# Hash attention and a squared-ReLU layer: the first pair's features moved behind the first sum, the last chunk's stores moved off Pool's queue

## The chip, the cores and the metric

The kernel runs on one core of a Trainium2 chip. The metric is the device time of one launch in microseconds (us). A core has engines that run side by side, each with its own instruction queue: TensorE (PE in the profile, its weight loads PEld), VectorE (DVE), ScalarE (ACT), GpSimd (POOL) and SyncE (SP, which only issues DMAs here). DMAs are issued from the queues of SP, ACT and POOL.

## The reference

Four batches of eight heads, 768 positions, head dimension 64. A query may see a key only if both have the same six-bit hash; the bits are the signs of six projections. The result, 3072 rows of 512, goes through a layer with 2048 hidden units and a squared ReLU.

```
q_bits = einsum('bhsd,dk->bhsk', q, proj) > 0          # and k_bits
q_bucket = sum(q_bits * 2**arange(6))                  # and k_bucket
mask = q_bucket[..., :, None] == k_bucket[..., None, :]
scores = where(mask, q @ k.T / 8, -1e9)
attn = exp(scores - max) / (sum + 1e-9);  x = (attn @ v) as (3072, 512)
h = x @ w_in                                           # (3072, 2048)
out = (relu(h) ** 2) @ w_out                           # (3072, 512)
```

## The kernel before

**Attention.** The 32 heads are worked in 16 pairs (two heads fill 128 partitions). For a pair, `features` (L330) turns the loaded queries and keys with two DVE transposes of 128x768; `hash_bits` (L337) multiplies them with the projections on PE, and `signs` (L351) makes bits of them with eight ACT instructions. `weigh` (L379) scales the key bits on ACT. Keys come in six tiles of 128. `score(pr, kt)` (L386) forms the products of bits and of features for one key tile on PE, in two column pieces (512 and 256), and ACT takes the exponential of each piece; `add_up` (L419) sums the exponentials on DVE; `attend` (L432) multiplies them with the values on PE. `finish` and `normalize` divide by the sums.

PSUM pieces for scores, hash products and totals come from one ring of three tiles (`turn`, L104), so a piece must be read by ACT before the third next one is begun. The exponentials lie in a ring of four. Beside all this, one weight piece after another is split and rounded to float32 (`part_weight`, `place_power`, `round_weight` on DVE and ACT).

The first pair differs from the others. Its features are PE transposes. The features of pair 1 are made in it, as there is no earlier pair to make them in, and its `prepare()` (hash products and signs of the next pair, L610) stands between score tiles; in later pairs `prepare` is called from `finish`, and the features of the pair after are made at the pair's start.

**The layer.** It runs in three chunks of 1024 rows (`NCH`, L66), with both matrix products done by Strassen-like schemes: seven products of half-size blocks in place of eight. For w_in, `hidden` and `hidden_pair` go through units. For w_out, `project` (L1050) runs seven outer products k = 0 to 6, each made by `product` (L699) with seven groups of matmuls on three accumulators. Within `product`, ACT copies an accumulator between groups (`keep`, L713: one, two, five, three): the copy `one` must have read accumulator 0 before PE adds the third group into it. The other groups' callbacks c11, c12, c22, c21 make the sums on DVE. At the first use of each weight factor a later one is loaded (`load_leaf`, L988, on ACT's queue).

**The output.** Outer product k = 5 (`sixth`, L1097) completes the output blocks (0, 1) and (1, 1), each in two halves (`close`, L1063), and k = 6 (`fourth`, L1105) block (1, 0). `put_out` (L1014) transposes a half on DVE and stores it with four DMAs of 32 partitions. Before the change block (1, 1) is stored from POOL's queue in every chunk, the others from SP's; in the last chunk POOL also takes two of the four stores of the first half of block (1, 0). The second half of that block in the last chunk goes another way (`put_last`, L1030: transposes on PE, stores from SP and ACT). After k = 5 of the last chunk `guard` (L762) decides whether the inputs need the general version that follows in the program; every engine reads its answer (L1278) and branches past that version.

The order of instructions on each engine is that of the program text (`tc.manual_schedule()`, L584); waits between engines and for DMAs are put in by the framework.

Of the kernel before, what the change touches and what calls it, by code (L numbers as in the profile page):

```python
# [34 lines left out]
def kernel(  # L35
# [10 lines left out]
    nc = tc.nc  # L46
# [20 lines left out]
    NCHUNK = B * S // NCH  # L67
# [36 lines left out]
    def turn(name):  # L104

        return ps_s.tile([P, 2, 512], FP32, name=name, tag="turn")
# [279 lines left out]
    def score(pr, kt):  # L386

        e = ring[len(weights) % NRING]
        weights[pr, kt] = e
        key = slice(kt * P, (kt + 1) * P)  # L390
        sts = []

        def products(st, lo, hi, src, first):
            for h in range(2):
                rows = slice(h * D, (h + 1) * D)
                nc.tensor.matmul(  # L396
                    out=st[:, h, 0:hi - lo], lhsT=src[pr, 1][rows, key],
                    rhs=src[pr, 0][rows, lo:hi], start=first, stop=not first,
                )


        if (pr, kt) == (0, 0):
            for lo, hi in CUTS:
                sts.append(turn("st"))
                products(sts[-1], lo, hi, feat, True)
        for i, (lo, hi) in enumerate(CUTS):
            if len(sts) <= i:
                sts.append(turn("st"))
                products(sts[i], lo, hi, bits, True)
                products(sts[i], lo, hi, feat, False)  # L410
            else:
                products(sts[i], lo, hi, bits, False)
            nc.scalar.activation(  # L413
                out=e[:, :, lo:hi], in_=sts[i][:, :, 0:hi - lo], func=ACTF.Exp, scale=scale
            )
# [3 lines left out]
    def add_up(pr, kt):  # L419

        if kt == 1:
            totals[pr] = p_n.tile([P, 2, S], FP32, name="total")
            nc.vector.scalar_tensor_tensor(
                out=totals[pr], in0=weights[pr, 0][:, :, 0:S], scalar=SB * TINY,
                in1=weights[pr, 1][:, :, 0:S], op0=ALU.add, op1=ALU.add,
            )
        else:
            nc.vector.tensor_tensor(  # L428
                out=totals[pr], in0=totals[pr], in1=weights[pr, kt][:, :, 0:S], op=ALU.add
            )  # L430

    def attend(pr, kt):  # L432
        if kt == 0:
            outs[pr] = ps_o.tile([P, 1024], FP32, name="xo")
        xo = outs[pr]
        for lo, hi in (CUTS[0], (CUTS[1][0], S + 1)):
            for h in range(2):
                nc.tensor.matmul(  # L438
                    out=xo[h * D:(h + 1) * D, lo:hi],
                    lhsT=nat[pr, "v_nat"][:, h, kt * D:(kt + 1) * D],  # L440
                    rhs=weights[pr, kt][:, h, lo:hi],
                    start=(kt == 0), stop=(kt == SB - 1),
                )
# [4 lines left out]
    def sum_up(pr, tot):  # L448


        tot = tot[:, 0]
        srcs = [totals[pr]] + [weights[pr, SB - 1]] * (pr in sums)
        for src in srcs:
            for c in range(2):
                for h in range(2):
                    g = 2 * h + c
                    nc.tensor.matmul(  # L457
                        out=tot[g * 32:(g + 1) * 32, 0:HS], lhsT=ones,
                        rhs=src[:, h, c * HS:(c + 1) * HS],
                        start=src is srcs[0], stop=src is srcs[-1],  # L460
                    )
        flip = p_n.tile([P, HS], FP32, name="flip")
        nc.vector.transpose(out=flip, in_=tot[:, 0:HS])
        once = p_n.tile([P, NB], FP32, name="once")
        nc.vector.reciprocal(
            out=once, in_=flip.rearrange("p (n f) -> p n f", f=32)[:, :, 0]
        )
        both = p_n.tile([P, 2, NB], FP32, name="both")
        nc.vector.tensor_tensor(
            out=both, in0=which,  # L470
            in1=once.rearrange("p (o n) -> p o n", o=1).to_broadcast([P, 2, NB]), op=ALU.mult,
        )
        onces[pr] = both

    def spread(pr):

        both = onces.pop(pr)
        rec = outs[pr][:, 1024 - 2 * NB:]
        for h in range(2):
            nc.tensor.matmul(  # L480
                out=rec[h * D:(h + 1) * D], lhsT=picks[:, h * D:(h + 1) * D],
                rhs=both.rearrange("p c n -> p (c n)"), start=True, stop=True,
            )
        recs[pr] = rec
# [58 lines left out]
    def load_x(i):  # L543

        x = p_c.tile([P, NFT, NCH], FP32, name="x")
        nc.gpsimd.dma_start(out=x, in_=x_all[:, :, i * NCH:(i + 1) * NCH])
        xs[i] = x, [p_c.tile([P, 2, NCH // 2], FP32, name=f"t_x{n}") for n in range(3)]
# [16 lines left out]
    def sum_x(i, n):  # L564

        x, (t1, t2, t3) = xs[i]
        lo, hi = slice(0, NCH // 2), slice(NCH // 2, NCH)
        b11, b12, b21, b22 = x[:, 0:2, lo], x[:, 0:2, hi], x[:, 2:4, lo], x[:, 2:4, hi]
        minus(*((t1, b12, b11), (t2, b22, t1), (t3, b22, b12), (b12, b21, t2))[n - 1])

    def finish(pr, beside=None):

        tot = turn("tot")
        if beside:
            beside()
        sum_up(pr, tot)
        if pr == NP - 1:
            sum_x(0, 2)
            sum_x(0, 3)
        for kt in (SB - 2, SB - 1):  # L580
            attend(pr, kt)
        spread(pr)

    with tc.manual_schedule():  # L584
# [21 lines left out]
        for pr in range(NP):  # L606
            a, b = 2 * pr, 2 * pr + 1
            more = pr + 1 < NP

            def prepare():  # L610

                hash_bits(pr + 1, turn("hash"))
                for w in (1, 0):
                    signs(pr + 1, w)


            if pr + 2 < NP:
                load_pair(pr + 2)
            if pr == X_0:
                load_x(0)  # L620
            if not more:
                sums_in(3)
            if more and pr > 0:
                for w in range(2):
                    features(pr + 1, w)
            if pr > 0:
                round_weight(b - 2)
                load_weight(b)
            score(pr, 0)
            if pr == 0:  # L630
                first_keys(1, turn("hash"))
            score(pr, 1)
            if pr == 0:
                for w in range(2):
                    features(1, w)
            if pr > 0:
                finish(pr - 1, prepare if more else None)
            add_up(pr, 1)
            if pr > 0:
                normalize(pr - 1)  # L640


            if pr == X_0 + 1:
                for n in range(2):
                    load_unit(n)
            part_weight(a)
            score(pr, 2)
            if pr == 0:
                prepare()
            score(pr, 3)  # L650
            if more and pr > 0:
                weigh(pr + 1)
            place_power(a)
            attend(pr, 0)
            attend(pr, 1)
            for kt in (2, 3):
                add_up(pr, kt)
            if more:
                load_values(pr + 1)


            round_weight(a)
            part_weight(b)
            if more:
                load_weight(a + 2)
            score(pr, 4)
            score(pr, 5)
            if pr == 0:
                weigh(1)
            place_power(b)  # L670
            attend(pr, 2)
            attend(pr, 3)
            add_up(pr, 4)

            if pr not in sums:
                add_up(pr, 5)
            if pr in sums:
                sums_in(sums[pr])
# [335 lines left out]
        def put_out(i, ih, jh, n, o):  # L1014


            ot = p_r.tile([P, HN], FP32, name="h", bufs=NH)
            nc.vector.transpose(out=ot, in_=o)
            m0 = ih * HD + n * P
            at = slice(i * NCH + jh * HN, i * NCH + (jh + 1) * HN)  # L1020
            for a in range(P // 32):
                queue = nc.gpsimd if (ih, jh) == (1, 1) else nc.sync
                if (i, ih, jh) == (NCHUNK - 1, 1, 0) and a % 2:
                    queue = nc.gpsimd
                queue.dma_start(
                    out=out[at, m0 + a * 32:m0 + (a + 1) * 32].rearrange("(c i) j -> i c j", i=32),
                    in_=ot[a * 32:(a + 1) * 32].rearrange("i (c j) -> i c j", j=32),
                )
# [451 lines left out]
```

## Time and profile before

| what | value |
|---|---|
| three runs | 882.09, 882.37, 883.88 us; median 882.37 |
| the profiled execution | 882.09 us, of it 880.2 us from the first to the last instruction |
| busy: PE, DVE, ACT, POOL | 866.6, 756.0, 391.7, 106.9 us |
| mean granted clock | 0.997 |
| attention | until about 334 us |
| three chunks of the layer | the rest |
| last matmul of the last product begins / last store is issued | 870.9 / 873.8 us |

In the profile's lines an instruction has its engine, its line in the kernel, the tile that it writes and the tiles that it reads, and in brackets the idle time of its engine before it with what ended that idle time. Busy time is not limit time: an engine can be busy with work that nobody waits for, and a wait costs only where the chain to the end runs through it.

### The profile page before, as it was taken

The numbers are of one execution on the slowest core, as the hardware profiler recorded it, in microseconds if no ns is written. First come the engines' busy times: TensorE is split into PE (matmuls) and PEld (weight loads), VectorE is DVE, ScalarE is ACT, GpSimd is POOL, SyncE is SP. The second block draws the span as 40 slices with busy tenths as digits, with TensorE's granted clock in tenths as the row PEclk, the third lists the DMA queues.
The fourth block names the chain that finished last, engine by engine and source line by source line (L and its number), as shares of the span: only waits on it lengthen the run. The fifth ranks groups of instructions, "written<-read, shape, count | busy, mean of one in ns | idle before, by whom it ended". The sixth has DMA issues, their size and how long they took to land.

```text
span 880.2 us, 12164 instructions
## 1 busy us (share of the span) xinstructions
PE 866.6 (98%) x4364; PEld 519.7 (59%) x4364; DVE 756.0 (86%) x1096; ACT 391.7 (45%) x673; POOL 106.9 (12%) x172
## 2 busy tenths in 40 slices
PE   8999999999999999999999999999999999999996
PEld 3444444444444444444688865556888755568885
DVE  5999999999999998888779968888889788888875
ACT  6988888888888851222211123332111233321110
POOL 2000000000000000564221021111000211110002
PEclk9999999999999999999999999999999999999998
DMA  9677779889777545989897765436846744355565
GB/s 175 149 144 134 198 183 190 181 275 206 158 166 188 160 137 199 301 260 289 283 355 249 180 160 174 162 117 228 287 145 188 170 159 156 128 167 151 161 175 104
DMA packets 224132, 167.09 MB, mean 190 GB/s; under 512 B 164449, under 2 KB 181345, under 8 KB 224065
## 3 DMA queue, kind: packets, MB, share of 16 engines
q1 hardware_dynamic: 189152, 87.19, 40.4%
q0 software_dynamic: 12528, 41.30, 15.0%
q10 hardware_dynamic: 22384, 37.76, 13.9%
q8 instruction: 36, 0.59, 0.3%
q14 instruction: 32, 0.25, 0.1%
HBM read 124.52 MB, written 41.68 MB: 189 GB/s over the span
## 4 chain that ended last, share of the span: by engine, by line
PE 94%; DVE 2%; ACT 1%; DMA 1%; issue 0%; ACTq 0%; DVEq 0%
PE acc L708 40%; PE st L396 17%; PE acc L927 16%; PE xo L438 13%; PE acc L880 5%; PE tot L457 2%; PE hash L346 2%; DVE total L428 1%; DMA k_nat<-in_k_dram 1%; ACT e L413 1%; ACT bits L356 1%; DMA w_in<-s_in 0%; DVE out_piece L179 0%; DVE power L171 0%; ACT small L160 0%
## 5 line engine op out<-in xcount | busy, mean ns | idle before, releaser
L413 ACT ACTIVATE e<-st 128x1024 f32<-128x1024 f32 x192 | 145.1, 810 | 46.8 <-PE st L396 42.7
L396 PE MATMUL st<-feat,feat 64*128 64x512 f32 (+1 forms) x768 | 150.4, 483 | 0.0
L438 PE MATMUL xo<-e,v_nat 128*64 128x512 f32 (+1 forms) x768 | 134.8, 492 | 0.0
L708 PE MATMUL acc<-b,leaf 128*128 128x256 f32 x600 | 133.3, 379 | 0.7 <-issue 0.7
L708 PEld LDWEIGHTS acc<-b,leaf 128*128 128x128 f32 x600 | 113.8, 190 | 17.2 <-issue 1.9
L428 DVE TENSOR_TENSOR total<-total,e 128x1536 f32<-128x1536 f32 x61 | 107.2, 1757 | 7.9 <-ACT e L413 3.6
L438 PEld LDWEIGHTS xo<-e,v_nat 128*64 128x64 f32 x768 | 51.3, 136 | 82.1 <-issue 75.0
L927 PE MATMUL acc<-t_x,w_unit 128*128 128x512 f32 x192 | 90.2, 592 | 0.0
L396 PEld LDWEIGHTS st<-feat,feat 64*128 64x128 f32 x768 | 66.0, 188 | 33.2 <-issue 23.9
L708 PE MATMUL acc<-t,leaf 128*128 128x256 f32 x336 | 76.2, 380 | 0.0
L356 ACT ACTIVATE bits<-hash,lifts 32x384 bf16<-32x384 f32 x120 | 68.7, 573 | 2.3 <-PE hash L346 0.5
L708 PEld LDWEIGHTS acc<-t,leaf 128*128 128x128 f32 x336 | 63.7, 190 | 9.1 <-DVE t L519 0.5
L792 DVE SCALAR_TENSOR_TENSOR b<-h 128x512 f32<-128x512 f32 x96 | 65.7, 691 | 3.0
L396 PE MATMUL st<-bits,bits 64*128 64x256 bf16 (+1 forms) x384 | 63.0, 325 | 1.7 <-ACT e L413 1.2
L927 PE MATMUL acc<-x,w_unit 128*128 128x512 f32 x128 | 60.1, 592 | 0.0
L708 PE MATMUL acc<-x,w_unit 128*128 128x512 f32 x128 | 56.6, 594 | 0.0
L708 PE MATMUL acc<-b_t,leaf 128*128 128x256 f32 x240 | 53.8, 379 | 0.0
L927 PEld LDWEIGHTS acc<-t_x,w_unit 128*128 128x128 f32 x192 | 36.5, 190 | 28.9 <-issue 26.8
L715 ACT COPY two<-acc 128x256 f32<-128x256 f32 (+1 forms) x29 | 12.5, 431 | 87.7 <-PE acc L708 66.0
L715 ACT COPY one<-acc 128x256 f32<-128x256 f32 (+1 forms) x29 | 12.5, 431 | 85.8 <-PE acc L708 42.9
L708 PEld LDWEIGHTS acc<-b_t,leaf 128*128 128x128 f32 x240 | 45.5, 190 | 6.2
L396 PEld LDWEIGHTS <-bits 64*128 64x128 bf16 x384 | 23.5, 93 | 42.1 <-issue 38.4
(161 smaller groups left out, 1169.7 us busy)
## 6 DMA issues: line engine op xcount, KB each, us to landing
leaf<-w_out ACTq DMA_DIRECT2D x142, 256.0 KB, 3.1
w_unit<-w_in SPq DMA_DIRECT2D x16, 640.0 KB, 4.0
raw<-in_moe_w_in_dram SPq DMA_DIRECT2D x16, 512.0 KB, 5.5
raw<-in_moe_w_out_dram SPq DMA_DIRECT2D x16, 512.0 KB, 4.4
w_unit<-w_in SPq DMA_DIRECT2D x8, 896.0 KB, 8.0
w_out<-sums POOLq DMA_DIRECT2D x16, 448.0 KB, 6.7
sum<-w_in SPq DMA_DIRECT2D x16, 448.0 KB, 4.7
v_nat<-in_v_dram SPq DMA_DIRECT2D x16, 384.0 KB, 4.5
```

Source lines behind the costliest of these rows:

```text
L346: nc.tensor.matmul(out=banks[g * NR_B:(g + 1) * NR_B, h, 0:HS], lhsT=projs[rows], rhs=feat[pr, w][rows, c * HS:(c + 1) * HS], start=True, ...
L356: nc.scalar.activation(out=t[h * D:h * D + NR_B, c * HS:(c + 1) * HS], in_=hashed[pr, w][at, h, 0:HS], func=ACTF.Sign, scale=HUGE, bias=li ...
L396: nc.tensor.matmul(out=st[:, h, 0:hi - lo], lhsT=src[pr, 1][rows, key], rhs=src[pr, 0][rows, lo:hi], start=first, stop=not first,)
L413: nc.scalar.activation(out=e[:, :, lo:hi], in_=sts[i][:, :, 0:hi - lo], func=ACTF.Exp, scale=scale)
L428: nc.vector.tensor_tensor(out=totals[pr], in0=totals[pr], in1=weights[pr, kt][:, :, 0:S], op=ALU.add)
L438: nc.tensor.matmul(out=xo[h * D:(h + 1) * D, lo:hi], lhsT=nat[pr, "v_nat"][:, h, kt * D:(kt + 1) * D], rhs=weights[pr, kt][:, h, lo:hi], s ...
L457: nc.tensor.matmul(out=tot[g * 32:(g + 1) * 32, 0:HS], lhsT=ones, rhs=src[:, h, c * HS:(c + 1) * HS], start=src is srcs[0], stop=src is sr ...
L708: nc.tensor.matmul(out=acc[to], lhsT=a(i), rhs=b(i), start=first and i == 0, stop=last and i == n - 1, skip_group_check=True,)
L715: nc.scalar.copy(out=t, in_=acc[of])
L792: nc.vector.scalar_tensor_tensor(out=out, in0=h, scalar=0.0, in1=h, op0=ALU.max, op1=ALU.mult)
L880: nc.tensor.matmul(out=out, lhsT=w[:, a], rhs=b, start=start, stop=stop, skip_group_check=True)
L927: nc.tensor.matmul(out=acc[to], lhsT=w[:, PLACE[a], f], rhs=bt[b](f), start=first and f == 0, stop=last and f == NFT // 2 - 1, skip_group_ ...
```

## The change

In the first pair (pr = 0) the two feature transposes of pair 1 move behind the first sum, `add_up(0, 1)`, and `prepare()` moves from between `score(0, 2)` and `score(0, 3)` to behind `score(0, 3)`. For other pairs the order stays what it was.

In the last chunk no output store is issued from POOL. For both blocks with `ih == 1`, row blocks a = 0 and 2 of each half are stored from SP's queue, a = 1 and 3 from ACT's. For block (1, 1) that moves eight stores: four to SP, four to ACT. For the first half of block (1, 0) it moves two from POOL to ACT.

```diff
             score(pr, 1)
+            if pr > 0:
+                finish(pr - 1, prepare if more else None)
+            add_up(pr, 1)
             if pr == 0:
                 for w in range(2):
                     features(1, w)
-            if pr > 0:
-                finish(pr - 1, prepare if more else None)
-            add_up(pr, 1)
             if pr > 0:
                 normalize(pr - 1)
...
             score(pr, 2)
+            score(pr, 3)
             if pr == 0:
                 prepare()
-            score(pr, 3)
-            if more and pr > 0:
+            elif more:
                 weigh(pr + 1)
...
                 queue = nc.gpsimd if (ih, jh) == (1, 1) else nc.sync
-                if (i, ih, jh) == (NCHUNK - 1, 1, 0) and a % 2:
-                    queue = nc.gpsimd
+
+                if i == NCHUNK - 1 and ih == 1:
+                    queue = (nc.sync, nc.scalar)[a % 2]
                 queue.dma_start(
```

## The prediction

> **What bounds the kernel now.** I read the page's busy table first, then busy time by stretch, then the timeline of each engine in the two places that the change touches: the first pair (12 to 36 us) and the last two products (855 to 880 us).
>
> ```profile
> PE 866.6 (98%) x4364; PEld 519.7 (59%) x4364; DVE 756.0 (86%) x1096; ACT 391.7 (45%) x673; POOL 106.9 (12%) x172
> ```
>
> ```profile
> 12.00:33.00 21.00, 19.29 (x147) 9.04 (x148) 17.17 (x20) 18.96 (x29) 0.00 (x0) 1.00 1.04 201
> 33.00:329.00 296.00, 296.00 (x2196) 135.73 (x2188) 277.79 (x339) 247.63 (x363) 0.91 (x1) 1.00 0.75 176
> ```
>
> Columns of the stretches: from, to, length, then busy time (and count) of PE, PEld, DVE, ACT, POOL, the granted clock, DMA share, GB/s. From 33 to 329 us PE is busy all the time. So whatever makes PE late in the first pair stays until the end, unless something there gives it back. The first pair, by the timelines of DVE, PE and ACT (start, length, engine, line, operation, the idle time before it and what ended it):
>
> ```profile
> 13.50 0.97 DVE L333 STREAM_TRANSPOSE feat<-q_nat 128x768 f32<-128x768 f32 x1
> 14.40 0.94 DVE L333 STREAM_TRANSPOSE feat<-k_nat 128x768 f32<-128x768 f32 x1
> 15.26 1.72 DVE L423 SCALAR_TENSOR_TENSOR total<-e,e 128x1536 f32<-128x1536 f32 x1
> ...
> 22.92 1.76 DVE L428 TENSOR_TENSOR total<-total,e 128x1536 f32<-128x1536 f32 x1 [3.60 <-ACT e L413]
> ```
>
> ```profile
> 15.57 0.88 PE L346 MATMUL hash<-feat,projs 64*32 64x384 f32 x16
> ...
> 21.40 0.39 PE L396 MATMUL st<-bits,bits 64*128 64x512 bf16 x2 [0.49 <-ACT bits L356]
> ...
> 25.26 0.28 PE L396 MATMUL st<-bits,bits 64*128 64x256 bf16 x2 [0.99 <-ACT e L413]
> ...
> 31.98 1.50 PE L346 MATMUL hash<-feat,projs 64*32 64x384 f32 x16
> ```
>
> ```profile
> 16.68 4.67 ACT L356 ACTIVATE bits<-hash,lifts 32x384 bf16<-32x384 f32 x8
> 21.37 1.51 ACT L413 ACTIVATE e<-st 128x1024 f32<-128x1024 f32 x2
> ```
>
> The reader sees that PE is ready for the next pair's hash products at 15.57 and the features are there at 15.34; that ACT then computes the signs for 4.67 us and is the engine that PE waits for, at 21.40 and 25.26; and that DVE has 3.60 us to spare before 22.92. At 31.98 the hash products of pair 2 take 1.50 us against 0.88 in the first pair: their second half waits for the key features.
>
> The last two products:
>
> ```profile
> 859.77 0.71 DVE L1018 STREAM_TRANSPOSE h<-o 128x512 f32<-128x512 f32 x1
> ...
> 863.92 0.71 DVE L1018 STREAM_TRANSPOSE h<-o 128x512 f32<-128x512 f32 x1
> ```
>
> ```profile
> 859.01 3.62 PE L708 MATMUL acc<-b_t,leaf 128*128 128x256 f32 x16
> 862.47 3.62 PE L708 MATMUL acc<-t,leaf 128*128 128x256 f32 x16
> ```
>
> ```profile
> 860.94 0.37 ACT L715 COPY one<-acc 128x256 f32<-128x256 f32 x1 [4.97 <-PE acc L708]
> ```
>
> ```profile
> 860.78 2.61 POOL L1025 DMA_DIRECT2D out_dram<-h  x4 [79.42 <-DVE h L1018]
> 864.93 2.57 POOL L1025 DMA_DIRECT2D out_dram<-h  x4 [1.54 <-DVE most L770]
> ```
>
> The eight block (1,1) stores of the last chunk are POOL's two groups. They start when DVE has transposed each half (860.48 and 864.63), which is 2 us and more behind PE: PE is in the seventh product from 859.01 on while DVE still forms the outputs of the sixth. POOL computes nothing then, so its waiting costs nothing. ACT in that time has one duty: the copy `one` (done at 861.31) without which PE may not add the third group of matmuls into the same accumulator at 862.47. That copy has 1.15 us to spare.
>
> One more row, from an earlier stage, shows how ACT treats a store in its queue:
>
> ```profile
> 774.72 2.26 ACTq L994 DMA_DIRECT2D leaf<-w_out  x5
> 777.02 0.59 ACT L935 COPY one<-acc 128x512 f32<-128x512 f32 x1 [1.72 <-DMA leaf<-w_out]
> ```
>
> Five DMA issues take 2.26 us, 0.45 each with the gap, and the copy behind them starts 0.04 us after the last. ACT works its queue in order, DMA issues included.
>
> **The change, part 1: features behind the first sum, hash products behind score(0, 3).** No instruction is added; two DVE transposes move past one sum, 16 matmul records, eight signs move past two exponentials. No DMA is moved past anything on SP or POOL. DVE: the first sum needs both exponentials of key tile 1. Four exponentials take 13.52 to 16.65, so those two are done at 15.03. The sum runs 15.07 to 16.79, the features 16.70 to 17.67 and 17.60 to 18.53, against 15.34 before. PE: score(0, 3) moves up to 15.57 and takes the 1.73 us that it took from 16.38 to 18.10, until 17.30. Then the hash products wait for the query features (0.4 us) and their key half for 18.53. By the pair-2 row, in which a late key half starts at 32.63 and the next work at 33.41, the next work (attend) comes 0.78 us after 18.59: at 19.37, where it was 18.10. So PE loses 1.27 there at once. ACT: the exponentials of tile 3 now run beside this, 16.86 to 18.39; that saves 1.51 behind the signs. But the signs start at 19.51 instead of 16.68 (2.83 later) and take 4.67, to 24.18; the weight placing (0.72 and 0.63) and the first exponential of tile 4 follow and end at 26.50 against 25.21. PE's wait, now 0.99 at 25.26, ends at 26.55: 1.29 late. That the two losses are alike is no sum: the second is what counts, the first lies before it. DVE: the weight rounding waits for ACT's placing, so the pair-2 features end at 33.61 against 32.58, 1.03 late. PE, 1.29 late, now finds the query features there and waits less for the key half: hash(2) is left 1.03 late. From 33 on PE is without a gap, so **+1.0** stays. Bounds: +1.3 if pair 2 gives nothing back; below, 0, if the signs' shift is covered by the 1.48 us of waits (0.49 and 0.99) that PE has there already.
>
> **Part 2: stores of the last chunk.** POOL loses ten of its issues (0.65 each, 6.5 us on an engine that nobody waits for): worth nothing. SP gains four: two behind its four stores that end at 860.95, two behind those of 863.15 to 865.77; its next store is due at 871.31, so about 1 us of issue is covered by 5 us. ACT gains six. Two, of the first half, wait for 860.48, with only leaf loads behind them; these leaves are used from 865.9 and 867.7 on and land about 3 us after issue, before PE needs them. Two, of the second half, wait for DVE until 864.63, and behind them stand a leaf load and the copy `one`. Working: 864.63 plus 0.03 (SP's reaction to the transpose before it: 863.12 to 863.15), plus three issues of 0.45 (the row of five), plus 0.04, is 866.06; the copy takes 0.37, PE reacts in 0.04: 866.47 against 862.47. **+4.0.** PE has then done the first two groups and has nothing else to do; everything after shifts with it, and DVE, which has caught up by 866.3, shortens nothing. If DVE had finished 3.5 us sooner there would be no stall. Bounds: 3.7 with issues of 0.33 (the shortest leaf issue). Above, 4.9 with two stores of 0.86 (the slowest SP store there), and 5.8 if the stores also wait for the SP stores ahead of them to land (863.15 plus the median 3.3 us to landing is 866.45).
>
> The last two of ACT's six follow the transpose that ends at 871.28. They are issued by 872.2, and ACT's next copy starts at 872.57 when PE has transposed: hidden by 0.3, costing up to 0.3 if they are slow. At the end, POOL's last two stores leave the DMA engines. Their queue fills 8.8% of the last 10.2 us, 0.9 us for each engine, ahead of the last four stores, which take 4.1 to 4.4 us to land. Two hardware-queue stores replace them, issued earlier. Between -0.9 and +0.3; I take **-0.3**.
>
> [...]
>
> **Sum:** 1.0 + 4.0 - 0.3 = +4.7. The profiled execution took 882.09 us (880.2 of span, 1.9 around it), so 886.8. The median shown, 882.37, is 0.28 above that execution; 0.2% is 1.8 us, about what these runs can tell from no change.
>
> **Rivals.**
> 1. *ACT isn't held* (the other side): the copy `one` passes the waiting stores, or these don't wait so long. For it: ACT is busy 1.86 of 17 us there. Against: the row of five. It decides if the copy can end by 862.47, that is if the stores are let go by about 860.7, when only the first half's transpose is done. Without the 4.0, +0.7: **882.8**, no change that can be told.
> 2. *The first pair costs nothing*: PE's 1.48 us of waits and DVE's 3.60 cover the shift. Against: ACT's chain of signs has no gap between 16.68 and 25.21. Sum +3.7: **885.8**.
> 3. *The stores on ACT wait longer*, for SP's stores to land or for slow issues. For it: SP's issues there reach 0.86. Sum with 5.8 for 4.0: +6.5, **888.6**.
>
> **How the numbers follow.** As summed 0.68; rival 1 0.08; rival 2 0.13; rival 3 0.09; a gain by anything else 0.02. Slower: 0.68 + 0.13 + 0.09 = 0.90; same: 0.07 of rival 1; faster: 0.03 (the rest, with a tail gain of 0.9 and more on top of rival 1). The likeliest case spans 885.3 to 888.0 by its bounds. The range takes in rivals 2 and 3 with the ends of the tail: 884.8 to 888.8, which leaves out rival 1 and little else.
>
> **What would show it.** In the first pair: total L423 at about 15.1, features to 18.5, signs from 19.5, PE's wait for `e` ending near 26.5, hash(2) left about 1 us late. Wrong if PE passes 33.41's place less than 0.5 us late. At the end: a gap of about 4 us in PE ahead of the third group of the seventh product, ended by ACT `one`, and two stores on ACT's queue right before that copy, starting with the end of the second transpose. Wrong if `one` starts with PE's first group, as before. If the gap is over 5 us, rival 3.

## The result and the profile after

| | before | after |
|---|---|---|
| median of six runs | 882.66 us (882.09 to 883.88) | 889.75 us (888.62 to 891.18) |
| the profiled execution, and its span | 882.09, 880.2 | 888.62, 886.9 |
| mean granted clock | 0.997 (profiled execution) | 0.993 to 0.995 (six runs) |

The change makes the kernel slower: ratio 1.0079, 95% interval 1.0066 to 1.0092, or 7.1 us. The forecast was +4.7 us, 886.8 us within 884.8 to 888.8; the measured median lies 0.95 us above the upper end. The profiled execution after is the fastest of its six runs, 1.1 us below their median, so the terms read from it below are those of a short run.

**The first pair.** From the timelines of DVE, PE and ACT of the kernel after (start, length, engine, line, operation, and the idle time before it with what ended it):

```profile
14.64 1.76 DVE L423 SCALAR_TENSOR_TENSOR total<-e,e 128x1536 f32<-128x1536 f32 x1 [1.48 <-ACT e L413]
16.32 0.97 DVE L333 STREAM_TRANSPOSE feat<-q_nat 128x768 f32<-128x768 f32 x1
17.21 0.94 DVE L333 STREAM_TRANSPOSE feat<-k_nat 128x768 f32<-128x768 f32 x1
```

```profile
17.43 1.62 PE L346 MATMUL hash<-feat,projs 64*32 64x384 f32 x16 [0.60 <-ACT e L413]
...
23.89 0.39 PE L396 MATMUL st<-bits,bits 64*128 64x512 bf16 x2 [0.38 <-ACT bits L356]
...
26.34 0.29 PE L396 MATMUL st<-bits,bits 64*128 64x256 bf16 x2 [1.21 <-ACT e L413]
...
34.08 0.85 PE L457 MATMUL tot<-total,ones 128*32 128x384 f32 x8
```

```profile
19.17 4.67 ACT L356 ACTIVATE bits<-hash,lifts 32x384 bf16<-32x384 f32 x8 [1.32 <-issue]
```

The features end at 18.15 and the signs begin at 19.17 and still take 4.67. PE's waits that end at 23.89 and 26.34 take 0.38 and 1.21, about as long as the two before (0.49 and 0.99, ending at 21.40 and 25.26). The first now stands one key tile later, ahead of tile 5 and not of tile 4; the second stands at the same place in the work and ends 1.1 us later. The totals of pair 1 begin at 34.08 against 33.41. In this execution the scores of key tile 1 began 0.42 earlier (11.81 against 12.23; PE's wait of 0.53 us for the load of `k_nat`, which stands in the trace before, is not in this one, and nothing of the change lies before them), so the first pair has lost 1.09. Between there and the guard's transposes at 859.51 (before 858.79) another 0.05 is added, and that is all for 825 us.

**The last two products.** PE and ACT, by their timelines:

```profile
859.73 3.62 PE L708 MATMUL acc<-b_t,leaf 128*128 128x256 f32 x16
867.61 5.41 PE L708 MATMUL acc<-t,leaf 128*128 128x256 f32 x16 [4.26 <-ACT one L715]
872.85 5.34 PE L708 MATMUL acc<-b_t,leaf 128*128 128x256 f32 x24
```

```profile
865.39 0.86 ACTq L1026 DMA_DIRECT2D out_dram<-h  x2
866.37 0.44 ACTq L994 DMA_DIRECT2D leaf<-w_out  x1
867.18 0.37 ACT L715 COPY one<-acc 128x256 f32<-128x256 f32 x1 [10.50 <-DMA out_dram<-h]
```

PE has done two groups of matmuls of the last product and then waits 4.26 us for the copy `one`. ACT has that copy behind two stores and a leaf load (the two stores of the first half, issued from 861.23 on, lie ahead of these and hold nobody). The stores begin at 865.39, 0.04 after DVE's transpose of the second half (864.64 to 865.35). The bracket of the last line names a DMA, but PE had written the copy's input by about 861.7 (before, the copy began 1.93 after PE's first group: 859.73 + 1.93), and it reads nothing of a DMA. It starts late because of what stands ahead of it in ACT's queue.

The second PE line holds what the forecast did not have: the same 16 matmul records of the third and fourth groups take 5.41 us, against 3.62 before. The stretches of this place (from, to, length, busy time and count of PE, PEld, DVE, ACT, POOL, the granted clock, DMA share, GB/s):

```profile
863.30:867.60 4.30, 0.05 (x1) 0.00 (x0) 3.62 (x8) 0.37 (x1) 0.00 (x0) 1.00 0.75 141
867.60:868.50 0.90, 0.89 (x4) 0.82 (x5) 0.84 (x2) 0.00 (x0) 0.00 (x0) 1.00 0.91 165
868.50:872.00 3.50, 3.50 (x11) 2.76 (x10) 0.00 (x0) 0.37 (x1) 0.00 (x0) 0.51 0.88 216
872.00:878.30 6.30, 6.20 (x29) 5.12 (x27) 1.66 (x4) 0.74 (x2) 0.00 (x0) 1.00 0.00 0
```

The granted clock is 1.00 while PE idles, stays so for the first 0.9 us of its new work, falls to half for 3.4 us and comes back. Before, it was 1.00 throughout this place.

**Where the time went**, span against span: start 0.42 earlier, first pair +1.09, between +0.05, the third group's start +4.42 (it would be 859.73 + 3.46 = 863.19, and is 867.61), groups three and four +1.79 (5.24 against 3.45 from start to start), tail -0.31 (7.06 against 7.37 from PE's last matmul to the end of the span). The sum is +6.62, which is the difference of the spans (886.86 and 880.24).

### The profile page after: what moved, and what is told of

It is laid out like the page before. It is cut to its first block, busy times and chain, and to the rows that moved or that the text cites. A ratio compares the mean times of both kernels' runs of the same rounds, so it can differ in the third digit from the quotient of the medians.

```text
span 886.9 us, 12166 instructions
## 1 busy us (share of the span) xinstructions
PE 869.1 (98%) x4364; PEld 521.0 (59%) x4364; DVE 756.2 (85%) x1096; ACT 391.8 (44%) x673; POOL 100.4 (11%) x162
## 4 chain that ended last, share of the span: by engine, by line
PE 94%; DVE 3%; ACT 1%; DMA 1%; issue 1%; DVEq 0%; ACTq 0%
PE acc L708 39%; PE st L396 17%; PE acc L927 15%; PE xo L438 13%; PE acc L880 5%; PE tot L457 2%; PE hash L346 1%; DVE total L428 1%; DMA out_dram<-h 1%; ACT e L413 1%; ACT bits L356 1%; PE xo L326 0%; DVE h L1018 0%; DMA w_in<-s_in 0%; DVE o L1004 0%
## 5 line engine op out<-in xcount | busy, mean ns | idle before, releaser
L708 PE MATMUL acc<-t,leaf 128*128 128x256 f32 x336 | 78.0, 386 | 4.3 <-ACT one L715 4.3
```

The lines of the kernel that those rows point to most:

```text
L708: nc.tensor.matmul(out=acc[to], lhsT=a(i), rhs=b(i), start=first and i == 0, stop=last and i == n - 1, skip_group_check=True,)
```

## The experiments

All times are medians, compared with runs of the kernel before on the same chip (882.3 to 882.9).

**1. The first pair alone**: the whole change, with the stores left as they were before.

```diff
-                if i == NCHUNK - 1 and ih == 1:
-                    queue = (nc.sync, nc.scalar)[a % 2]
+                if (i, ih, jh) == (NCHUNK - 1, 1, 0) and a % 2:
+                    queue = nc.gpsimd
```

> The first pair's reordering alone, stores as before. Theory (first pair 1.1 us, ACT held 4.4, clock at half 1.8, tail -0.2): 882.7 + 1.1 = 883.8 us; hash(2) ends 1.1 us late counted from the start of score(0, 1); no gap in PE in the seventh product, granted clock 1.00 until PE's last matmul. Rival (the first pair costs nothing, all 7 us come from the stores): 882.7.

Measured 884.03 us, ratio 1.0017 (1.0008 to 1.0027), +1.3. From the scores of key tile 1 to pair 1's totals it takes 22.27 us (21.18 before), +1.09, as in the whole change. PE has no gap in the last product, and its third and fourth groups take 3.62 us, as before.

**2. The stores alone**: the kernel before with the new store queues.

```diff
-                if (i, ih, jh) == (NCHUNK - 1, 1, 0) and a % 2:
-                    queue = nc.gpsimd
+                if i == NCHUNK - 1 and ih == 1:
+                    queue = (nc.sync, nc.scalar)[a % 2]
```

> The stores' move alone, first pair as before. Theory: 882.7 + 4.4 + 1.8 - 0.2 = 888.7 us, with a PE gap of about 4.3 us ahead of the third group of the seventh product and 3.4 us at a granted clock of 0.5 after it. Rival (the first pair holds the larger part): under 886.

Measured 888.86 us, ratio 1.0069 (1.0052 to 1.0085), +6.2. PE's timeline, and the stretch behind the gap:

```profile
867.24 6.68 PE L708 MATMUL acc<-t,leaf 128*128 128x256 f32 x16 [4.25 <-ACT one L715]
```

```profile
867.20:873.20 6.00, 5.96 (x14) 4.79 (x15) 0.85 (x2) 0.37 (x1) 0.00 (x0) 0.50 0.66 152
```

The gap is that of the whole change. Here the clock is 0.50 over all of the 6.00 us behind the gap, against 3.41 us in the whole change. The two groups take 6.52 us from start to start, 3.07 more than at full clock.

**3. The gap filled.** If the half clock comes from PE's idling, spare work in the gap must prevent it without moving anything else. Five fp32 matmuls of 128x512 into a spare accumulator, read by nobody, go ahead of the third group of the last product.

```diff
+            if fill:
+                fill()
             c11(acc[1], one)
             add(0, at(4), bt["t2"], False, False)
...
+                void = ps_t.tile([P, 512], FP32, name="acc3")
+                for _ in range(NFILL):
+                    nc.tensor.matmul(
+                        out=void, lhsT=ident, rhs=xs[i][0][:, 0, 0:512], start=True, stop=True
+                    )
```

> The whole change, and five spare fp32 matmuls of 128x512 (0.86 us each by the rows of that shape, 4.3 us in all) on PE ahead of the third group of the last product, into an accumulator that nobody reads, so that PE is busy while ACT is held. Theory (the halved clock follows from the idle gap): ACT one ends at the same place, no granted clock under 1.00 before PE's last matmul, the third and fourth group in 3.6 us, 889.75 - 1.8 = 888.0 us. Rival (the slow matmuls have another cause: DMA traffic of the stores and leaf loads, or the clock falling near the end by itself): still 5.4 us for these groups, 889.7.

Measured 887.59 us (887.54 to 888.05), ratio 1.0058 (1.0042 to 1.0075). PE's timeline, and the stretch:

```profile
863.79 4.45 PE L1116 MATMUL acc<-x,ident 128*128 128x512 f32 x10
868.21 3.72 PE L709 MATMUL acc<-t,leaf 128*128 128x256 f32 x16
```

```profile
868.00:872.00 4.00, 4.00 (x19) 3.35 (x19) 0.85 (x2) 0.53 (x2) 0.00 (x0) 1.00 1.04 232
```

The third group starts as late as in the whole change (8.10 us after the guard's transposes in both), the clock stays at 1.00, and the two groups take 3.72 us (3.55 from start to start, 1.69 less than in the whole change). The kernel is 2.2 us faster than the change by medians, with more work in it. The stores and leaf loads are those of the whole change, so DMA traffic isn't the cause. This is the term that the forecast lacked, isolated: PE's idling cost its idle time and then slow matmuls behind it.

**4. A shorter gap.** The kernel before, with two stores of the second half of block (0, 1) moved from SP to ACT; they have less to wait for.

```diff
                     queue = nc.gpsimd
+                if (i, ih, jh, n) == (NCHUNK - 1, 0, 1, 1) and a % 2:
+                    queue = nc.scalar
```

> The kernel before, but the two odd stores of the second half of block (0, 1) in the last chunk go to ACT's queue; their transpose ends 1.5 us before that of block (1, 1). Theory (a held copy one, and the half clock only after a gap long enough): PE gap of 2.6 us in place of 4.3; if that is short of what halves the clock, no clock below 1.00 before PE's last matmul and 882.7 + 2.7 = 885.4 us. Rival (any PE gap of this kind halves the clock for one stretch of 3.4 us): 887.1.

Measured 887.74 us, ratio 1.0067 (1.005 to 1.0084).

```profile
867.07 3.72 PE L708 MATMUL acc<-t,leaf 128*128 128x256 f32 x16 [3.29 <-ACT one L715]
```

```profile
867.00:870.60 3.60, 3.53 (x16) 3.14 (x17) 1.20 (x3) 0.39 (x2) 1.64 (x3) 1.00 0.95 247
```

PE's timeline shows the gap: it was 3.29 and not 2.6, as the leaf load behind the stores took 1.17 us to issue. In this profiled execution (886.78 us, mean clock 0.997) the clock stayed at 1.00 behind the gap, and the two groups take 3.72 us. The three others took 887.15, 888.32 and 889.2 us with mean clocks of 0.995, 0.995 and 0.993. A half clock behind the gap would fit these, but they have no profile, and experiment 5 has a mean of 0.994 with groups of 3.62 us and a long tail, so it is not shown. The median lies nearer to the rival's 887.1 than to the 885.4.

**5. Block (1, 1) all on SP**, so that no store with a long wait stands on ACT.

```diff
-                    queue = (nc.sync, nc.scalar)[a % 2]
+                    queue = nc.sync if jh == 1 else (nc.sync, nc.scalar)[a % 2]
```

> The whole change, but block (1, 1) of the last chunk goes to SP's queue alone; ACT keeps the two stores of block (1, 0). Theory (only the stores that stand ahead of the copy one cost anything): no PE gap, clock 1.00, 882.7 + 1.1 - 0.2 = 883.6 us. Rival (taking POOL off the stores costs by itself, SP's queue being late for block (1, 0)): 885 or more, SP's last stores over 1 us later than DVE's transpose.

Measured 889.07 us, ratio 1.0074 (1.0057 to 1.0091). The timelines of ACT and PE, then the waits of SP's queue (waiting line, what it waited for, us in total, times, longest):

```profile
863.24 0.37 ACT L715 COPY one<-acc 128x256 f32<-128x256 f32 x1 [4.97 <-PE acc L708]
```

```profile
864.76 3.62 PE L708 MATMUL acc<-t,leaf 128*128 128x256 f32 x16
```

```profile
SPq L1026 <- DMA out_dram<-h: 7.2, 2, 6.9
```

The copy is on time and PE's gap is gone, as expected, but the kernel is no faster: the span ends 12.41 us after PE's last matmul in place of 7.06. The second half of block (1, 1) was ready for SP's stores at 866.93, when DVE had transposed it. By the row, SP's queue stood 6.9 us in one wait until a store to `out_dram` had landed; SP's two last stores were issued from 879.94 to 882.20 (before, from 872.97 to 873.81). In the trace before, SP's queue has no wait for a store from 850 us on. Why it waits for one here was not shown. The rival's 885 or more came true, with this wait; whether the loss of POOL has a share in it was not shown. My total for this run, 883.6, missed by 5.5 us, of which 5.0 stand in the tail (12.41 - 7.37).

**6. Three ways to give ACT's stores to POOL**: its four of block (1, 1); its two of that block's second half only; all six.

```diff
-                    queue = (nc.sync, nc.scalar)[a % 2]
+                    queue = (nc.sync, nc.gpsimd if jh == 1 else nc.scalar)[a % 2]
```
```diff
-                    queue = (nc.sync, nc.scalar)[a % 2]
+                    queue = (nc.sync, nc.gpsimd if (jh, n) == (1, 1) else nc.scalar)[a % 2]
```
```diff
-                    queue = (nc.sync, nc.scalar)[a % 2]
+                    queue = (nc.sync, nc.gpsimd)[a % 2]
```

> The whole change, but ACT's four stores of block (1, 1) go to POOL's queue, which stands ahead of no other work; SP's share stays, and ACT keeps its two stores of block (1, 0). Theory (the loss is in the stores ahead of the copy one on ACT): no PE gap, granted clock 1.00 to PE's last matmul, no new wait on SP, 882.7 + 1.1 - 0.2 = 883.6 us. Rival (any thinning of POOL's share makes SP late at the end, as where SP took all of block (1, 1)): SP's stores end later than 876, 886 or more.

> The whole change, but of ACT's stores of block (1, 1) only the two of the second half go to POOL; the two of the first half stay on ACT. Theory (ACT is held until DVE's transpose of the half that it stores): the first half's transpose ends 4.15 us sooner than the second's, so the copy one ends at about 863.6 against 863.2 needed: a PE gap of 0.3 to 0.8 us, clock 1.00, 883.6 + 0.5 = 884.1 us. Rival (the number of DMA issues on ACT counts, not the half): half of the 4.4 us and some of the clock's loss, 886 or more.

> The whole change, but all six stores that it gives to ACT go to POOL's queue instead (block (1, 0) is then as before, block (1, 1) shared by SP and POOL). Theory (the 1.5 us that stayed when only ACT's share of block (1, 1) went to POOL come from SP's stores of block (1, 0) waiting for ACT's stores of that block to land): no PE gap and no such wait on SP, 7.4 us from PE's last matmul to the end as before, 882.3 + 1.2 = 883.5 us. Rival (SP's larger share of block (1, 1) makes the end later by itself): 885 again.

| on POOL | time | ratio | PE's gap | last matmul to end |
|---|---|---|---|---|
| four of (1, 1) | 885.32 us | 1.0037 (1.0023 to 1.0051) | none | 8.80 |
| two of (1, 1) | 885.49 us | 1.0036 (1.0022 to 1.0051) | 0.35 | 8.52 |
| all six | 887.13 us | 1.0054 (1.0038 to 1.0069) | none | 10.65 |

With the second half's two stores off ACT, the gap is 0.35 at most, and the third and fourth groups take 3.62 to 3.72 us. All three still miss what I expected, and by their tails. In the first SP's queue waited 6.1 us for a store to land, in the second 1.9 and 1.6 (longest waits of two rows). After these two I held that it was ACT's stores of block (1, 0), first half, whose landing SP waits for, but taking them away too made it worse. There the waits of SP's queue show:

```profile
SPq L1046 <- DMA out_dram<-h: 4.2, 1, 4.2
```

SP's two last stores, of that block's second half, are issued from 874.51 to 879.40, 4.89 us against 0.84 before. So with ACT's other stores gone SP's queue still waited for a store to land, now at another line; what decides which store waits was not shown. With the tail's 3.3 us (10.65 - 7.37) the sum is 882.7 + 1.1 + 3.3 = 887.1, the measured time.

**7. The same stores on ACT, but behind its last copy.** ACT's four stores of block (1, 1) are issued behind the copy `three` of the last product.

```diff
+                if (i, ih, jh) == (NCHUNK - 1, 1, 1) and a % 2:
+                    later.append(store)
+                else:
+                    store()
...
+                if n == 1:
+                    while later:
+                        later.pop(0)()
```

> The whole change, with ACT's four stores of block (1, 1) still on ACT's queue but issued behind the copy three of the last product in place of ahead of the copy one. Theory (what stands behind the waiting store decides, not the engine): no PE gap, clock 1.00 to PE's last matmul, 882.7 + 1.1 - 0.3 = 883.5 us if no store waits for another's completion semaphore at the end, up to 887 if one does. Rival (issuing stores from ACT in this stage costs by itself): a gap in PE or a late copy two or three, over 887.

Measured 885.24 us, ratio 1.0026 (1.0014 to 1.0037). ACT's timeline at the copy, and the waits of SP's queue:

```profile
863.09 0.37 ACT L715 COPY one<-acc 128x256 f32<-128x256 f32 x1 [4.97 <-DMA out_dram<-h]
```

```profile
SPq L1029 <- DMA out_dram<-h: 4.3, 1, 4.3
SPq L1053 <- DMA out_dram<-h: 1.6, 1, 1.6
```

No gap, and the third and fourth groups take 3.62 us: with the same stores on the same engine the kernel is 4.5 us faster than the change. So it is the place in ACT's queue that cost PE its time, not the use of ACT for stores. What remains over the first pair's 1.1 goes with SP's waits for stores to land, 4.3 and 1.6 us (tail 8.48).

**8. Only the hash products moved** behind score(0, 3), and **9. only the features moved** behind the first sum.

```diff
             score(pr, 2)
+            score(pr, 3)
             if pr == 0:
                 prepare()
-            score(pr, 3)
```
```diff
-            if pr == 0:
-                for w in range(2):
-                    features(1, w)
             if pr > 0:
                 finish(pr - 1, prepare if more else None)
             add_up(pr, 1)
+            if pr == 0:
+                for w in range(2):
+                    features(1, w)
```

> The kernel before with only the hash products and signs moved behind score(0, 3); the features stay ahead of the first sum, the stores as before. Theory (the features decide, since the hash products wait for them): the hash products need not wait, tile 3's exponentials run 1.5 us earlier and the signs 1.7 later, 882.7 + 0.2 = 882.9 us, no PE wait ahead of the hash products. Rival (moving the hash products is itself the loss, through ACT's later signs): 883.8, with PE's wait for e ending 1.1 us later than before.

> The kernel before with only the feature transposes moved behind the first sum; hash products and signs stay between score(0, 2) and score(0, 3), the stores as before. Theory (the hash products wait for the later features, and with them score(0, 3) and its exponentials, which stand behind the signs on ACT): PE waits about 3 us ahead of the hash products, its wait for e ends 2.9 us late, DVE's second pair of features 3 us late: 882.3 + 2.9 = 885.2 us. Rival (the late features cost the 1.1 us of the whole change and no more): 883.4.

Measured 882.64 us, ratio 1.0004 (0.9994 to 1.0013), and 886.06 us, ratio 1.0039 (1.0024 to 1.0054). With the features late and nothing put ahead of the hash products, PE's timeline and a stretch behind the gap read:

```profile
17.73 2.27 PE L346 MATMUL hash<-feat,projs 64*32 64x384 f32 x16 [2.21 <-DVE feat L333]
```

```profile
18.40:21.90 3.50, 3.50 (x18) 1.00 (x16) 2.36 (x4) 1.74 (x4) 0.00 (x0) 0.51 0.60 97
```

The cost to pair 1's totals is 3.54, more than I expected, and again work at half clock stands in it: a mean of 0.51 over these 3.50 us, in which PE is busy throughout. In the whole change score(0, 3) fills that wait: the gap ahead of the hash products is 0.60. The two moves don't add up (0 and 3.5 alone, 1.1 together), since the second one covers most of what the first one opens.

**10. Pair 1's key bits on DVE** instead of ACT, in the kernel before, to shorten the chain of signs that both orders wait for.

```diff
-                hash_bits(pr + 1, turn("hash"))
+                banks = turn("hash")
+                hash_bits(pr + 1, banks)
+                if pr == 0:
+                    bits[1, 1] = all_bits[1][1]
+                    for c in range(2):
+                        key_bits(1, c, banks)
+                    signs(1, 0)
+                    return
...
-            part_weight(a)
             score(pr, 2)
             if pr == 0:
                 prepare()
+            part_weight(a)
...
-            if pr == 0:
-                weigh(1)
```

> The kernel before with the key bits of pair 1 made on DVE, as those of the first pair are, in place of four of the eight signs and the scaling on ACT; features, hash products and stores as before. Theory (in the first pair ACT's signs are what PE waits for, and DVE has 3.6 us to spare): PE's waits of 0.49 and 0.99 us go, 882.3 - 1.4 = 880.9 us. Rival (DVE is made late by the 3 us more and hands it on by the second pair's features): 882.3 or more.

Measured 883.56 us, ratio 1.0010 (1.0001 to 1.0019): the 880.9 was missed, there is no gain. ACT is left with four signs, which take 2.32 us, but they wait for DVE, which reads the same PSUM tile first (ACT's timeline):

```profile
19.98 2.32 ACT L356 ACTIVATE bits<-hash,lifts 32x384 bf16<-32x384 f32 x4 [3.16 <-DVE bits L374]
```

PE's first wait grew with it, from 0.49 to 1.28 us, and the second stayed at 0.99.

No version tried here is faster than the kernel before.

## Why the prediction was right in part and its range wrong

**The first pair: right.** Forecast +1.0, measured +1.09. The first sum, the features, the signs and the ends of PE's waits for the features and for `e` stand within 0.5 us of where they were put, in the order that was given. Rival 2 (it costs nothing) is out by experiment 1.

**ACT held by the stores: right.** Forecast 4.0 between 3.7 and 5.8, measured 4.42. Experiments 2, 5, 6 and 7 show it from four sides. Rival 1 is out. Of the working, two stores and the leaf load came out at 1.42 us from the first issue to the end of the third (forecast 1.35). The copy then began 0.37 after the leaf load and not 0.04, which is most of the term's error of 0.4. The 0.37 is the same in experiments 2 and 3, and about 0.1 in experiments 4 and the second of 6; what it is stays open.

**The tail: right.** Forecast -0.3, measured -0.31. The tail is 7.06, 7.10 and 7.14 us in the three traces with these store queues (after, experiments 2 and 3) and 7.26 to 7.39 in the five with those of before; that POOL's share of the DMA engines makes the difference was argued and is not tested. It was right for this assignment of stores alone: the five others tried (experiments 5, 6 and 7) have tails from 8.48 to 12.41, with a wait of SP's queue (1.6 to 6.9 us) that I had not looked for.

**What failed** is the step "everything after shifts with it": the shift was taken as the gap's length, and slower work behind the gap was put at nothing. The gap's length is one cost. The other is that the matmuls behind it ran at half clock for 3.4 us in the profiled execution, +1.8, and for 6.0 us in experiment 2's, +3.1. Filling the gap took it away (experiment 3). With the measured terms the sum is 1.1 + 4.4 + 1.8 - 0.3 = 7.0, against 7.1 by the medians; that they meet so closely is in part luck, as the terms are those of the fastest run. Of the 2.95 us between 886.8 and the measured 889.75, 1.8 is the half clock and 0.4 ACT's longer hold; 0.57 is the starting point, as the sum began at the profiled execution's 882.09, and the median of six runs before is 882.66.

Rival 3, which ends close to the measured time, is not thereby right: it needed a longer wait of ACT, and the gap stayed below the 5 us set for it; the stores began 0.04 behind DVE's transpose. Two slips in the working change nothing of this: by its own numbers DVE would have had to finish 4.0 us sooner, not 3.5, for no stall (866.47 - 862.47), and rival 3 with the tail's +0.3 ends at 889.2, above the stated 888.8.

The trace before has no gap of this kind in a busy PE with work behind it; the nearest, PE's own waits of 0.5 and 1.0 in the first pair, had clock 1.00 behind them, and none of the bounds held anything for the work behind the gap. But it shows the clock fall with PE idle, behind PE's last matmul, which ends at 872.87:

```profile
872.18:875.59 3.41, 0.69 (x4) 0.32 (x4) 0.62 (x2) 0.37 (x1) 0.68 (x2) 1.00 0.80 157
875.60:879.01 3.41, 0.00 (x0) 0.00 (x0) 0.00 (x0) 0.00 (x0) 0.00 (x0) 0.50 0.08 18
```

That is the fault: a new idle time of some 4 us was priced as a pure delay, although the clock fell in this trace 2.73 us after PE had stopped.

**What the clock did behind each gap.** PE's gaps by its timelines, and the granted clock of stretches at or behind them:

| trace | PE's gap (us) | stretch (us) | granted clock |
|---|---|---|---|
| after | 4.26, to 867.61 | 867.60 to 868.50 | 1.00 |
| after | the same | 868.50 to 872.00 | 0.51 |
| after | the same | 872.00 to 878.30 | 1.00 |
| experiment 2 | 4.25, to 867.24 | 867.20 to 873.20 | 0.50 |
| experiment 3 | filled | 868.00 to 872.00 | 1.00 |
| experiment 4 | 3.29, to 867.07 | 867.00 to 870.60 | 1.00 |
| experiment 9 | 2.21, to 17.73 | 18.40 to 21.90 | 0.51 |
| before | 0.49 and 0.99, to 21.40 and 25.26 | 12.00 to 33.00 | 1.00 |

The length of the gap does not sort these cases: behind 2.21 us there was work at half clock, behind 3.29 us there was none, and behind 4.26 and 4.25 us it lasted 3.41 and 6.00 us. What decides it was not shown. The runs after lie between 888.62 and 891.18, those with the gap filled between 887.54 and 888.05; that this is half clock of a different length from run to run is a guess, as one run of each has a profile. For the trace after, 3.41 us at half clock should cost a busy PE half of that, by my estimate 1.7 us, and 1.79 was measured.

## What to carry to other kernels

Look at what comes next behind a DMA in a computing engine's queue, and who needs it, before counting issue times: here two waiting stores and a leaf load ahead of the copy `one` on ACT cost 4.42 us, and the same stores behind the copy `three` left no gap in PE (experiment 7). A new gap of some microseconds in a PE that was busy all along can cost more than its length: behind gaps of 4.26 and 4.25 us (after, experiment 2) work at half clock added 1.8 and 3.1 us, behind one of 2.21 us (experiment 9) the clock was 0.51, and behind one of 3.29 us (experiment 4) it stayed at 1.00. When stores are moved between SP and ACT at the end of a kernel, read what each queue then waits for: here SP's stood up to 6.9 us in one wait for a store to land.

## What the runs showed of the hardware that was not expected

- After a gap of 4.26 us PE's granted clock stayed at 1.00 for 0.9 us of new work and only then was halved, for 3.41 us (after); in experiment 2, behind a gap of 4.25 us, it was 0.50 from the start of the new work on, for 6.00 us. A gap of 3.29 us had no halving in the profiled execution of experiment 4, one of 2.21 us had it (0.51 over 3.50 us, experiment 9).
- SP's queue waited for stores to land, up to 6.9 us in one wait (experiment 5), 6.1, 1.9 and 4.2 us in the three of experiment 6 and 4.3 us in experiment 7. The tails of these five are 8.48 to 12.41 us, those of the others 7.06 to 7.39.
- In the last two products a leaf load's issue on ACT took 0.33 to 1.17 us, the longest behind two stores (experiment 4).
